# One instruction per pair of heads for the score maxima and the exponentials, on one PSUM tile; a third pair of W2 tiles split earlier

## The chip, the cores and the metric

The kernel runs on one core of a Trainium2 chip. The metric is device time in microseconds (us) of one execution; lower is better. Before the change it is 2239.94 us, the median of three runs between 2239.41 and 2240.25.

## What is computed

Two branches share one input and are mixed per token by a sigmoid gate: softmax attention with 32 heads of 18 channels, and an MLP with a hidden width of 4608.

```python
x = A_x                                            # (1, 2048, 576), float32
g = sigmoid((x * gate_w).sum(-1, keepdims=True))
q, k, v = heads(x @ wqkv)                          # 32 heads, Dh = 18
p = softmax(q @ k.T * 18 ** -0.5)
a = merge(p @ v) @ wo
b = gelu(layernorm(x) @ w1 + b1) @ w2 + b2         # 576 -> 4608 -> 576
out = g * a + (1 - g) * b
```

## The kernel before

**Three stages.** The entry stage (about 0 to 235 us) transposes x, forms the scores' operands q and k (`qk_group`) and v (`v_group`), stores them in DRAM scratch, and writes the normalised x for the MLP. It also runs the first rounds of score maxima and prepares the first MLP weights. The main loop (to about 2163 us) is attention, with the whole MLP cut into small pieces between its matmuls. A short end projects the attention output with `wo` and adds the gated MLP rows.

**The attention loop.** Heads are taken in 16 pairs and queries in halves, which makes 32 units of 16 steps, 512 steps in all. A matmul needs at most 64 of the array's 128 rows here, so the two heads of a pair lie in the upper and the lower rows, and their matmuls run side by side. Below, a *pair* is such a couple of score matmuls, head 0 then head 1, each writing 512 columns, one PSUM bank. A step issues four pairs in turn: `s2` (keys by queries, L271, whose scores ACT turns into exponentials, L275), `s1` (queries by keys for the unit after next, L226, whose row maxima DVE takes, L228), and the same again. Every two to four steps `pv` (L291) multiplies the stored exponentials by v in one burst. Between the pairs lie pieces of the MLP: `h_pair` (L539, hidden units) and `out_pair` (L627, output rows). Reading a bank out, by the maximum or the exponential, is called its *evacuation* below: only after it may the bank be written again.

**What sets the order.** The program's order on each engine is fixed when it is built. `half_round`, `fill` and `turn_ends` place pieces by nominal costs (231 and 131 ns a step), `run_due` releases work that `defer` has put off by so many slots, and the list `bg` holds weight splits, each of which starts once its load should have landed: `LOADED` is the slot of the load plus `LAND`. Each engine then runs its own list in order and waits on semaphores that the builder inserts wherever two accesses to the same memory must not be exchanged.

**PSUM.** There are eight banks. `score_bank` hands the score matmuls a ring of five in the loop (three of `ps_s1`, two of `ps_s2`) and of four in the entry stage (three of `ps_s1`, one of `ps_o`). `ps_w` has two for the MLP, `ps_o` one for the output of `pv`, `ps_a` four in the entry stage. Each bank is a tile of its own. With five banks and two for each pair, a matmul's bank was last used two or three pairs earlier: in the built program the nearest evacuation that a pair of score matmuls waits for is that of two pairs back for 2012 of the 2048 pairs.

**Weights.** `split` rounds a loaded W1 or W2 tile (ACT, L402, L403, L405) and subtracts the rounded part from it (POOL, called from `pool_op`, L179), so that two reduced-precision matmuls give a float32 product. The parts go to scratch, and later token blocks read them from there (`reload`, L421). W1 and W2 are split in the first token block; `prep` and `prep_w2` ask for it.

Of the kernel before, what the change touches and what calls it, by code (L numbers as in the profile page):

```python
# [8 lines left out]
F32 = mybir.dt.float32  # L9
F32R = mybir.dt.float32r  # L10
AF = mybir.ActivationFunctionType
ALU = mybir.AluOpType
# [20 lines left out]
GC0 = 1.0 / 0.044715  # L33
LN_EPS = 1e-5
HALF = S // 2
NS1 = 3
LEAD = 4
FILL = 1250.0
SLOT = 950.0
# [27 lines left out]
def gated_mix_kernel(ctx: ExitStack, tc: tile.TileContext, x, wqkv, wo, w1, b1, w2, b2, gate_w, out):  # L67
# [32 lines left out]
    pp = ctx.enter_context(tc.tile_pool(name="pp", bufs=2))  # L100
    hp = ctx.enter_context(tc.tile_pool(name="hp", bufs=6))
    asm = ctx.enter_context(tc.tile_pool(name="asm", bufs=2))
    ps_s1 = ctx.enter_context(tc.tile_pool(name="ps_s1", bufs=NS1, space=PSUM))
    ps_o = ctx.enter_context(tc.tile_pool(name="ps_o", bufs=1, space=PSUM))
    QA = [att.tile([P, HALF], F32R, name=f"qa{i}") for i in range(3)]
    KA = [att.tile([P, S], F32R, name=f"ka{i}") for i in range(2)]
    VT = [att.tile([P, NT, VW], F32, name=f"vt{i}") for i in range(2)]
# [1 line left out]
    V0 = att.tile([P, NT, VW], F32, name="v0")  # L109
    oe = att.tile([P, TB], F32, name="oe")  # L110

    def psum(pool):
        return pool.tile([P, TB], F32, name="ps")

    ring = [0]

    def score_bank():

        ring[0] += 1
        if not looped[0]:  # L120
            return psum(ps_s1 if ring[0] % (NS1 + 1) < NS1 else ps_o)
        return psum(ps_s1 if ring[0] % (NS1 + 2) < NS1 else ps_s2)

    def big_tile():
        return yp.tile([P, 9, TB], F32R, name="big")
# [62 lines left out]
    def unit(u):  # L188
        return UNITS[u]
# [26 lines left out]
    def s1_round(u, r):  # L216


        t, kb = (r % 8, r // 8) if u in (0, NU - 3) else divmod(r, 4)
        if r == 0:  # L220
            M4[u] = asm.tile([P, 2, 8, 4], F32, name="m4")
        qa, ka = QA[u % 3], KA[unit(u)[0] % 2]
        for h in range(2):
            r0 = 64 * h
            ps = score_bank()
            nc.tensor.matmul(ps, qa[r0:r0 + 54, t * P:(t + 1) * P], ka[r0:r0 + 54, kb * TB:(kb + 1) * TB],  # L226
                             start=True, stop=True)
            nc.vector.tensor_reduce(M4[u][:, h, t, kb:kb + 1], ps, axis=AX.X, op=ALU.max)  # L228

    def s1_finish(u):  # L230

# [31 lines left out]
    def s2(u, kc, qb):  # L263
        qa, ka = QA[u % 3], KA[unit(u)[0] % 2]
        n = u * NT + kc
        if n < 2 and qb == 0:
            RING.insert(n, pp.tile([P, 2, 2, TB], F32, name="p"))
        ps = [score_bank() for _ in range(2)]
        for h in range(2):
            r0 = 64 * h  # L270
            nc.tensor.matmul(ps[h], ka[r0:r0 + 56, kc * P:(kc + 1) * P], qa[r0:r0 + 56, qb * TB:(qb + 1) * TB],  # L271
                             start=True, stop=True)
        def exps():
            for h in range(2):
                nc.scalar.activation(p_of(n)[:, qb, h], ps[h], AF.Exp, scale=SCALE)  # L275
        return exps

    OB = {}
# [1 line left out]
    def pv(n, m):  # L280

        u, kc = divmod(n, NT)
        if kc == 0:
            OB[u] = psum(ps_o)
        v = v_of(unit(u)[0])
        for c in range(n, n + m):
            for qb in range(2):
                for h in range(2):
                    r = 32 * (2 * h + qb)
                    k = c % NT  # L290
                    nc.tensor.matmul(OB[u][r:r + 32, :], v[:, k, 19 * h:19 * h + 32], p_of(c)[:, qb, h, :],  # L291
                                     start=(k == 0), stop=(k == NT - 1))
        if kc + m == NT:
            o_store(u, OB.pop(u))
# [45 lines left out]
    def mlp():  # L340
# [26 lines left out]
        def load_w1(q):  # L367

            if (1, q) in LOADED or q >= NQ0:
                return  # L370
            LOADED[1, q] = slot[0] + LAND
            f0 = 2 * q * P
            raw = raw1(q)
            for h in range(2):
                src = w1[256 * h:256 * h + 256, f0:f0 + 2 * P].rearrange("(c p) n -> p c n", p=64)
                nc.sync.dma_start(raw[64 * h:64 * h + 64, 0:8].rearrange("p (c j) n -> p c (j n)", j=2), src)
            for h in range(2):
                for j in range(2):
                    f1 = f0 + (j ^ h) * P
                    nc.sync.dma_start(raw[64 * h:64 * h + 64, 8 + j], w1[512:576, f1:f1 + P])  # L380

        def load_w2(c):
            if (2, c) in LOADED or c >= NFC:
                return
            LOADED[2, c] = slot[0] + LAND
            nc.sync.dma_start(raw2(c), w2[c * P:(c + 1) * P, :])

        def rounded(dst, src):
# [58 lines left out]
        room = [6]  # L447
        w2_next = [0]

        def prep_w2(upto):  # L450

            late = 0
            while room[0] and w2_next[0] < 2 * min(upto, npair):
                q, j = divmod(w2_next[0], 2)
                w2_next[0] += 1
                if last_of(of[q][0]) and q >= npair - 3 and q < npair - 1:
                    continue
                room[0] -= 1
                c = 2 * (q % NQ0) + j
                if q >= NQ0:  # L460
                    defer(late, lambda q=q, j=j, c=c: reload(W2, (q, j), wp2, [P, 2, D], w2_scr[c]))
                    late += 2
                    continue
                split(W2, (q, j), wp2, [P, 2, D], (2, c), raw2(c), w2_scr[c],
                      lambda c: load_w2(c + 2))
# [48 lines left out]
        def h_pair(q, inner=False):  # L514
# [6 lines left out]
                yield 0  # L521
            wh, wl = ready(W1, q)
            del W1[q]
            ps = [psum(ps_w) for _ in range(2)]
# [79 lines left out]
        def out_pair(i, t, acc):  # L604
# [4 lines left out]
            ps = [psum(ps_w) for _ in range(2)]  # L609
            steps = 12 * size  # L610
            ends = turn_ends(steps, steps // 2, {4: 1.5})
            k = 0
# [97 lines left out]
        for i in range(n + 1):  # L710
            q = first_of[i] if i < n else 0
            if i < n:
                yield from pair(q)
            if i > 0:
                if i == n:
                    between = {}
                elif last_of(i) and seq[i][2] > 2:
                    between = {0: pair(q + 1), 1: pair(q + 2, inner=True)}
                else:
                    between = {0 if seq[i][2] == 2 else 1: pair(q + 1)}  # L720
                was = held[0]
# [48 lines left out]
    with ExitStack() as a:  # L770
        wpool = a.enter_context(tc.tile_pool(name="a_w", bufs=1, side="right"))
        sm = a.enter_context(tc.tile_pool(name="a_sm", bufs=2, side="right"))
        ps_a = a.enter_context(tc.tile_pool(name="ps_a", bufs=4, space=PSUM))

        qkstack = ExitStack()
        wqk = qkstack.enter_context(tc.tile_pool(name="a_wqk", bufs=1))
# [41 lines left out]
                eng.tensor_tensor(lo[:, cs], raw[:, cs], hi[:, cs].bitcast(F32), op=ALU.subtract)  # L818

        def transposed(tb, c):  # L820
            ps = psum(ps_a)
# [66 lines left out]

        def stat_rows(tb):

            ps = psum(ps_a)
# [47 lines left out]
        def qk_group(tb, mt):  # L939
            big = xT[tb]  # L940
            wh, wl = W_QK
            ms = slice(mt * P, (mt + 1) * P)
            ps = psum(ps_a)
            k = 0
            for c in range(4):
                for w_, s_ in ((wh, c), (wh, 4 + c), (wl, c)):
# [12 lines left out]
        def v_group(tb, t, n, between=None):  # L959
# [4 lines left out]
            ps = psum(ps_a)  # L964
            k = 0
            for c in range(4):
                for s_, w_ in ((c, wh), (c, wl), (4 + c, wh)):
# [36 lines left out]
        for tb in range(NB):  # L1004
            work = [(qk_group, (tb, mt)) for mt in (range(9) if tb < 2 else (4, 0, 1, 2, 3, 5, 6, 7, 8))] + [(v_group, (tb, t, n)) for t in range(4) for n in range(2)]
            for g, (fn, args) in enumerate(work):
# [35 lines left out]
                if tb == NB - 1:  # L1042
                    if g == 0:
                        next(stream[0])
                    if g == 1:
                        load_k(0, 3 * TB, S)
                    if g == 2:
                        load_q(1)
                        next(stream[0])
                    if g == 9:  # L1050
                        qkstack.close()
                        wp1 = mstack.enter_context(tc.tile_pool(name="m_w1", bufs=3))
                        wp2 = mstack.enter_context(tc.tile_pool(name="m_w2", bufs=6))
                        next(stream[0])
                    if g == 7:
                        ps = psum(ps_a)
                        nc.tensor.transpose(ps[:, :NFC], b1r, ident[:NFC, :NFC])
                        nc.vector.tensor_copy(b1t, ps[:, :NFC])
                if tb == 1 and g == 5:
# [30 lines left out]
    def out_proj():  # L1090
# [171 lines left out]
        for b in range(NB):  # L1262
# [6 lines left out]
            for t in range(4):  # L1269
# [5 lines left out]
                res = io.tile([P, D], F32, name="res", bufs=6)  # L1275
                for n in range(2):
                    cs = slice(n * ND, (n + 1) * ND)
                    ps = psum(ps_w)
                    k = 0
                    for c in range(5):  # L1280
                        while done[b] <= c:
# [125 lines left out]
```

## Time and profile before

| | |
|---|---|
| median of the runs | 2239.94 us |
| the profiled execution | 2238.79 us |
| its span, first to last instruction | 2237.0 us |
| PE (TensorE matmul) busy | 99% of the span |
| DVE (VectorE) busy | 72% |
| ACT (ScalarE) busy | 63% |
| POOL (GpSimd) busy | 45% |
| mean TensorE clock granted | 0.994 |

The span is 1.8 us shorter than the profiled execution's own time, and that time lies 1.15 us under the median. In the profile's rows PEld is TensorE's weight load, SP the engine that issues most DMAs, and L226 line 226 of the kernel above. A matmul's end is modelled, so a busy PE isn't PE at its peak; starts are recorded.

### The profile page before, as it was taken

What the parts mean: (1) busy time and instruction counts of PE and PEld (TensorE: products, weight loads), DVE (VectorE), ACT (ScalarE), POOL (GpSimd) and SP (SyncE); (2) the same over time, 40 slices, a digit from 0 to 9 for tenths busy, and PEclk for the clock granted to TensorE, in tenths of its full rate; (3) what the DMA queues carried; (4) which work ended last, traced back from release to release, by engine and by line L of the source; (5) the groups of instructions that cost most, each with busy time, mean ns of one, the idle gap of its engine ahead of it and who ended that gap; (6) DMA issues with size and microseconds to landing.
All of it is one profiled execution on the core that took longest, in us unless ns stands there. A gap on an engine that the chain in (4) does not pass through costs nothing.

```text
span 2237.0 us, 51358 instructions
## 1 busy us (share of the span) xinstructions
PE 2204.4 (99%) x20496; PEld 1620.0 (72%) x20496; DVE 1619.0 (72%) x2816; ACT 1418.5 (63%) x2636; POOL 1005.0 (45%) x1017
## 2 busy tenths in 40 slices
PE   8999999999999999999999999999999999999999
PEld 7877666767677777777767677777677777777768
DVE  6675766777777777777777777777777777777734
ACT  4323866767776666666765676666666666667672
POOL 4322765556554525434543452543535354254600
PEclk9999999999999999999999999999999999999999
DMA  8857646444453522342341533243344324323355
GB/s 265 273 205 240 216 149 191 148 152 157 145 166 120 181 101 97 125 138 94 125 138 58 171 142 111 91 141 125 107 131 156 118 85 150 110 91 124 124 171 167
DMA packets 162041, 324.36 MB, mean 145 GB/s; under 512 B 65830, under 2 KB 85218, under 8 KB 151074
## 3 DMA queue, kind: packets, MB, share of 16 engines
q1 hardware_dynamic: 159494, 317.61, 44.1%
q8 instruction: 161, 2.64, 0.5%
q10 hardware_dynamic: 2244, 3.45, 0.4%
q14 instruction: 78, 0.64, 0.1%
q0 software_dynamic: 64, 0.02, 0.0%
HBM read 228.62 MB, written 96.69 MB: 145 GB/s over the span
## 4 chain that ended last, share of the span: by engine, by line
PE 86%; DMA 4%; DVE 4%; POOL 2%; issue 2%; SPq 1%; ACT 1%; POOLq 0%; ACTq 0%; DVEq 0%
PE ps L291 19%; PE ps L627 19%; PE ps L539 18%; PE ps L271 12%; PE ps L226 10%; PE ps L947 3%; PE ps L1284 2%; DVE m L228 2%; DMA x<-in_B_w_dram 1%; PE ps L968 1%; POOL zz L179 1%; POOL w L179 1%; DMA bt<-b_scr 1%; SPq L380 1%; DMA x<-ot_scr 0%
## 5 line engine op out<-in xcount | busy, mean ns | idle before, releaser
L228 DVE TENSOR_REDUCE m<-ps 128x1 f32<-128x512 f32 x2048 | 1302.5, 684 | 450.7 <-PE ps L226 428.8
L275 ACT ACTIVATE p<-ps 128x512 f32<-128x512 f32 x1048 | 567.5, 597 | 305.8 <-PE ps L271 277.3
L275 ACT ACTIVATE ring<-ps 128x512 f32<-128x512 f32 x1000 | 542.4, 596 | 273.1 <-PE ps L271 263.7
L539 PE MATMUL ps<-big,w 64*128 64x512 f32 x3888 | 612.7, 393 | 0.2 <-issue 0.2
L179 POOL TENSOR_SCALAR zz<-zz 128x512 f32<-128x512 f32 x288 | 178.2, 619 | 726.3 <-ACT zz L599 670.9
L271 PE MATMUL ps<-qa,ka 56*128 56x512 f32 x2048 | 474.2, 421 | 6.7 <-ACT ring L275 3.0
L226 PE MATMUL ps<-ka,qa 54*128 54x512 f32 x2048 | 461.1, 403 | 7.4 <-DVE m L228 7.3
L539 PEld LDWEIGHTS ps<-big,w 64*128 64x128 f32 x3888 | 412.1, 187 | 51.4 <-DMA big<-y_scr 0.5
L179 POOL TENSOR_TENSOR zz<-zz,z 128x512 f32<-128x512 f32 x288 | 371.2, 1289 | 24.0
L271 PEld LDWEIGHTS ps<-qa,ka 56*128 56x128 f32 x2048 | 220.8, 185 | 198.2 <-DVE m L228 124.0
L627 PE MATMUL ps<-w,hh 64*128 64x288 f32 x2752 | 317.9, 296 | 1.2 <-DMA w<-w_scr 1.2
L627 PEld LDWEIGHTS ps<-w,hh 64*128 64x128 f32 x2752 | 277.8, 188 | 15.7 <-POOL zz L179 1.0
L226 PEld LDWEIGHTS ps<-ka,qa 54*128 54x128 f32 x2048 | 245.9, 185 | 39.0 <-DVE m L228 14.2
L291 PE MATMUL ps<-p,vt 128*32 128x512 f32 x1968 | 240.7, 597 | 0.0
L627 PE MATMUL ps<-w,big 64*128 64x288 f32 x2496 | 234.0, 294 | 3.4 <-ACT w L405 2.5
L627 PE MATMUL ps<-w,hl 64*128 64x288 f32 x1376 | 233.1, 294 | 0.0
L291 PE MATMUL ps<-ring,vt 128*32 128x512 f32 x1872 | 231.3, 596 | 0.0
L627 PEld LDWEIGHTS ps<-w,big 64*128 64x128 f32 x2496 | 218.7, 188 | 13.9 <-ACT w L405 2.8
L179 POOL TENSOR_TENSOR w<-x,w 128x1024 fp32r<-128x1024 f32 (+1 forms) x72 | 101.3, 1429 | 211.7 <-ACT w L402 120.2
L627 PEld LDWEIGHTS ps<-w,hl 64*128 64x128 f32 x1376 | 159.3, 187 | 0.2
L291 PEld LDWEIGHTS ps<-p,vt 128*32 128x32 f32 x1968 | 54.5, 109 | 116.3 <-issue 107.9
L291 PEld LDWEIGHTS ps<-ring,vt 128*32 128x32 f32 x1872 | 52.5, 109 | 115.1 <-issue 115.1
(126 smaller groups left out, 1715.8 us busy)
## 6 DMA issues: line engine op xcount, KB each, us to landing
w<-w_scr SPq DMA_DIRECT2D x54, 1152.0 KB
w<-w_scr SPq DMA_DIRECT2D x108, 576.0 KB
w_scr<-w SPq DMA_DIRECT2D x18, 1152.0 KB
w_scr<-w SPq DMA_DIRECT2D x36, 576.0 KB
qa<-qk_scr SPq DMA_DIRECT2D x192, 72.0 KB
ka<-qk_scr SPq DMA_DIRECT2D x84, 144.0 KB
x<-in_B_w_dram SPq DMA_DIRECT2D x36, 288.0 KB
qk_scr<-hh SPq DMA_DIRECT2D x36, 256.0 KB
```

The lines of the kernel that those rows point to most:

```text
L179: fn(*args, **kw)
L226: nc.tensor.matmul(ps, qa[r0:r0 + 54, t * P:(t + 1) * P], ka[r0:r0 + 54, kb * TB:(kb + 1) * TB], start=True, stop=True)
L228: nc.vector.tensor_reduce(M4[u][:, h, t, kb:kb + 1], ps, axis=AX.X, op=ALU.max)
L271: nc.tensor.matmul(ps[h], ka[r0:r0 + 56, kc * P:(kc + 1) * P], qa[r0:r0 + 56, qb * TB:(qb + 1) * TB], start=True, stop=True)
L275: nc.scalar.activation(p_of(n)[:, qb, h], ps[h], AF.Exp, scale=SCALE)
L291: nc.tensor.matmul(OB[u][r:r + 32, :], v[:, k, 19 * h:19 * h + 32], p_of(c)[:, qb, h, :], start=(k == 0), stop=(k == NT - 1))
L380: nc.sync.dma_start(raw[64 * h:64 * h + 64, 8 + j], w1[512:576, f1:f1 + P])
L539: mm = nc.tensor.matmul(ps[nn], w_[r, 2 * c + nn if c < 4 else 8], y, start=(k == 0), stop=(k == 26))
L627: mm = nc.tensor.matmul(ps[nn][:, :ND], h_[r, tok], w_[p_][r, cs[nn]], start=(k == 0), stop=(k == steps - 1))
L947: nc.tensor.matmul(ps, w_[:, c, ms], big[:, s_, :], start=(k == 0), stop=False)
L968: nc.tensor.matmul(ps[:, :ND], big[:, s_, tok], w_[:, c, cs], start=(k == 0), stop=False)
L1284: nc.tensor.matmul(ps[:, :ND], OT[b][2][:, s_, tok], w_part(w_, c)[:, cs], start=(k == 0), stop=(k == 13))
```

## The change

All of PSUM becomes one tile of eight banks, `PS`, and a table says which banks each use takes in turn. `score_banks` takes the next two banks of the ring and returns them as one strided slice, with the lower bank first. In the loop the ring is 0, 1, 2, 3, 4, so the slices are (0,1), (2,3), (0,4), (1,2), (3,4), and then (0,1) again; in the entry stage they are (0,1) and (2,5). `s1_round` takes both heads' maxima in one reduce of 2 x 512 elements, `s2` both heads' exponentials in one activation. The names of the pools and the rings change accordingly; the lines move down by one or two.

In the weights, `prep_w2(3)` adds the third pair of W2 tiles to those split in the entry stage, a load in the loop counts as landed four slots later, and in the last group of a token block the reloads of W2 are one slot apart, not two.

```diff
-    ps_s1 = ctx.enter_context(tc.tile_pool(name="ps_s1", bufs=NS1, space=PSUM))
-    ps_o = ctx.enter_context(tc.tile_pool(name="ps_o", bufs=1, space=PSUM))
+    PS = ctx.enter_context(tc.tile_pool(name="ps", bufs=1, space=PSUM)).tile([P, 8, TB], F32, name="ps")
...
-    def score_bank():
-
-        ring[0] += 1
-        if not looped[0]:
-            return psum(ps_s1 if ring[0] % (NS1 + 1) < NS1 else ps_o)
-        return psum(ps_s1 if ring[0] % (NS1 + 2) < NS1 else ps_s2)
+    BANKS = {"s": (0, 1, 2, 5), "a": (3, 4, 6, 7), "o": (5,), "w": (6, 7)}
+    given = {}
+
+    def bank(use):
+
+        given[use] = given.get(use, -1) + 1
+        return BANKS[use][given[use] % len(BANKS[use])]
+
+    def psum(use):
+        return PS[:, bank(use)]
+
+    def score_banks():
+
+        lo, hi = sorted((bank("s"), bank("s")))
+        return PS[:, lo:hi + 1:hi - lo]
...
+        ps = score_banks()
         for h in range(2):
             r0 = 64 * h
-            ps = score_bank()
-            nc.tensor.matmul(ps, qa[r0:r0 + 54, t * P:(t + 1) * P], ka[r0:r0 + 54, kb * TB:(kb + 1) * TB],
+            nc.tensor.matmul(ps[:, h], qa[r0:r0 + 54, t * P:(t + 1) * P], ka[r0:r0 + 54, kb * TB:(kb + 1) * TB],
                              start=True, stop=True)
-            nc.vector.tensor_reduce(M4[u][:, h, t, kb:kb + 1], ps, axis=AX.X, op=ALU.max)
+        nc.vector.tensor_reduce(M4[u][:, :, t, kb], ps, axis=AX.X, op=ALU.max)
...
-        ps = [score_bank() for _ in range(2)]
+        ps = score_banks()
...
-            for h in range(2):
-                nc.scalar.activation(p_of(n)[:, qb, h], ps[h], AF.Exp, scale=SCALE)
+            nc.scalar.activation(p_of(n)[:, qb], ps, AF.Exp, scale=SCALE)
...
-            LOADED[1, q] = slot[0] + LAND
+            LOADED[1, q] = slot[0] + LAND + 4 * looped[0]
...
-            LOADED[2, c] = slot[0] + LAND
+            LOADED[2, c] = slot[0] + LAND + 4 * looped[0]
...
-        def prep_w2(upto):
+        def prep_w2(upto, apart=2):
...
-                    late += 2
+                    late += apart
...
         prep_w2(2)
         prep(2)
+        prep_w2(3)
...
-                    prep_w2(first_of[i] + seq[i][2] + 2 * (seq[i][0] == 0 and not last_of(i)))
+                    prep_w2(first_of[i] + seq[i][2] + 2 * (seq[i][0] == 0 and not last_of(i)), 1 if last_of(i) else 2)
...
-    ps_s2 = ctx.enter_context(tc.tile_pool(name="ps_s2", bufs=2, space=PSUM))
-    ps_w = ctx.enter_context(tc.tile_pool(name="ps_w", bufs=2, space=PSUM))
+    BANKS["s"] = (0, 1, 2, 3, 4)
+    given["s"] = -1
```

The order of PE's matmuls is the same in both programs, instruction by instruction. What differs on PE is what they wait for. The first place is PE in the loop, at 743.4 to 745 us of the profile of before: a pair of `s1`, a pair of `s2` and a pair of `s1`, with pieces of `out_pair` between. `ps` is a score bank, `hh` and `hl` are the parts of a hidden tile, and `[waits ...]` names the engine whose count the instruction waits for. Before:

```order
L226 MATMUL ps<-ka_108,qa_105 128x512 [waits Activation_49]
L226 MATMUL ps<-ka_108,qa_105 128x512 [waits DVE_49]
L627 MATMUL ps<-w_9559,hh 128x288 x4
L627 MATMUL ps<-w_9559,hl 128x288 x2
L271 MATMUL ps<-qa_107,ka_108 128x512 [waits DVE_49]
L271 MATMUL ps<-qa_107,ka_108 128x512 [waits Activation_49]
```

And in the changed program:

```order
L228 MATMUL ps<-ka_106,qa_103 128x512 [waits DVE_49]
L228 MATMUL ps<-ka_106,qa_103 128x512
L628 MATMUL ps<-w_7780,hh 128x288 x4
L628 MATMUL ps<-w_7780,hl 128x288 x2
L273 MATMUL ps<-qa_105,ka_106 128x512 [waits DVE_49]
L273 MATMUL ps<-qa_105,ka_106 128x512 [waits Activation_49]
```

No matmul has moved. The first `s1` pair here has the banks (0,4), the `s2` pair after it the banks (1,2). Before, the count for which the first L271 waits was that of the reduce three pairs back; now the count for which the first L273 waits is reached only by the reduce of the `s1` pair just ahead of it, the one that reads the slice (0,4). Such a wait, for the evacuation of the pair immediately ahead, stands before 392 of the 2048 pairs of the changed program, each time where a pair in (1,2) follows one in (0,4); before it stood before 10.

The second place is DVE at the same part of the loop, its reduces (`m` is the tile of maxima) and the sums of `out_pair`. Before:

```order
L228 TENSOR_REDUCE m_9806<-ps 128x1 [waits PE_49] x8
L640 SCALAR_TENSOR_TENSOR x<-ps,x 128x288 [waits PE_49] x2
L228 TENSOR_REDUCE m_9806<-ps 128x1 [waits PE_49] x6
```

And now:

```order
L230 TENSOR_REDUCE m_7974<-ps 128x2 [waits PE_49]
L641 SCALAR_TENSOR_TENSOR x<-ps,x 128x288 [waits PE_49] x2
L230 TENSOR_REDUCE m_7974<-ps 128x2 [waits PE_49,Activation_49] x2
L230 TENSOR_REDUCE m_7974<-ps 128x2 [waits PE_49]
L230 TENSOR_REDUCE m_7974<-ps 128x2 [waits PE_49,Activation_49]
```

Two reduces have become one, and some of them now wait for ACT as well as for PE. In 378 reduces that count is reached only by the exponential of the pair immediately ahead, and 377 exponentials wait likewise for the reduce of the pair ahead; before, a score evacuation waited for no evacuation on the other engine. In the entry stage 17 groups (of `qk_group`, `v_group` and the transposes, in the banks 3 and 4) wait for the reduce of a pair in (2,5).

The third place is POOL at the end of the entry stage, its share of the weight splits (`x` the loaded tile, `w` the rounded one: 128x576 a W2 tile, 128x1024 and 128x128 a W1 tile). Before:

```order
L179 TENSOR_TENSOR w_2278<-x,w_2278 128x1024
L179 TENSOR_TENSOR w_2278<-x,w_2278 128x128
L179 TENSOR_TENSOR w_2453<-x,w_2453 128x1024
L179 TENSOR_TENSOR w_2453<-x,w_2453 128x128
L179 TENSOR_SCALAR zz<-zz 128x512
```

And now:

```order
L181 TENSOR_TENSOR w_2065<-x,w_2065 128x1024
L181 TENSOR_TENSOR w_2065<-x,w_2065 128x128
L181 TENSOR_TENSOR w_2133<-x,w_2133 128x576
L181 TENSOR_TENSOR w_2164<-x,w_2164 128x576
L181 TENSOR_TENSOR w_2213<-x,w_2213 128x1024
L181 TENSOR_TENSOR w_2213<-x,w_2213 128x128
```

Two W2 subtractions have come forward, ahead of the third W1 tile; their two ACT roundings, two loads and two stores have come with them. In the first token block most later W2 splits stand one GELU piece further back than before.

More of the change, by code (lines that the diff above doesn't have):

```diff
@@ L35 @@
 HALF = S // 2
-NS1 = 3
 LEAD = 4
@@ L110, in gated_mix_kernel @@
     oe = att.tile([P, TB], F32, name="oe")
-    def psum(pool):
-        return pool.tile([P, TB], F32, name="ps")
-    ring = [0]
-    def score_bank():
-        ring[0] += 1
-        if not looped[0]:
-            return psum(ps_s1 if ring[0] % (NS1 + 1) < NS1 else ps_o)
-        return psum(ps_s1 if ring[0] % (NS1 + 2) < NS1 else ps_s2)
+    BANKS = {"s": (0, 1, 2, 5), "a": (3, 4, 6, 7), "o": (5,), "w": (6, 7)}
[8 more added lines that the diff above has]
+        return PS[:, lo:hi + 1:hi - lo]
     def big_tile():
@@ L267, in s2 @@
             RING.insert(n, pp.tile([P, 2, 2, TB], F32, name="p"))
-        ps = [score_bank() for _ in range(2)]
+        ps = score_banks()
         for h in range(2):
             r0 = 64 * h
-            nc.tensor.matmul(ps[h], ka[r0:r0 + 56, kc * P:(kc + 1) * P], qa[r0:r0 + 56, qb * TB:(qb + 1) * TB],
+            nc.tensor.matmul(ps[:, h], ka[r0:r0 + 56, kc * P:(kc + 1) * P], qa[r0:r0 + 56, qb * TB:(qb + 1) * TB],
                              start=True, stop=True)
         def exps():
-            for h in range(2):
-                nc.scalar.activation(p_of(n)[:, qb, h], ps[h], AF.Exp, scale=SCALE)
+            nc.scalar.activation(p_of(n)[:, qb], ps, AF.Exp, scale=SCALE)
         return exps
@@ L283, in pv @@
         if kc == 0:
-            OB[u] = psum(ps_o)
+            OB[u] = psum("o")
         v = v_of(unit(u)[0])
@@ L523, in h_pair @@
             del W1[q]
-            ps = [psum(ps_w) for _ in range(2)]
+            ps = [psum("w") for _ in range(2)]
             change = tb + 1 < NB and (q + 1) % NQ0 == 0
@@ L608, in out_pair @@
             cs = [slice(nn * ND, (nn + 1) * ND) for nn in range(2)]
-            ps = [psum(ps_w) for _ in range(2)]
+            ps = [psum("w") for _ in range(2)]
             steps = 12 * size
@@ L772, in gated_mix_kernel @@
         sm = a.enter_context(tc.tile_pool(name="a_sm", bufs=2, side="right"))
-        ps_a = a.enter_context(tc.tile_pool(name="ps_a", bufs=4, space=PSUM))
         qkstack = ExitStack()
@@ L820, in transposed @@
         def transposed(tb, c):
-            ps = psum(ps_a)
+            ps = psum("a")
             for t in range(4):
@@ L889, in stat_rows @@
         def stat_rows(tb):
-            ps = psum(ps_a)
+            ps = psum("a")
             nc.tensor.transpose(ps[:, :P], stp, ident)
@@ L942, in qk_group @@
             ms = slice(mt * P, (mt + 1) * P)
-            ps = psum(ps_a)
+            ps = psum("a")
             k = 0
@@ L963, in v_group @@
             wh, wl = W_V
-            ps = psum(ps_a)
+            ps = psum("a")
             k = 0
@@ L1055, in gated_mix_kernel @@
                     if g == 7:
-                        ps = psum(ps_a)
+                        ps = psum("a")
                         nc.tensor.transpose(ps[:, :NFC], b1r, ident[:NFC, :NFC])
@@ L1277, in out_proj @@
                     cs = slice(n * ND, (n + 1) * ND)
-                    ps = psum(ps_w)
+                    ps = psum("w")
                     k = 0
```

## The prediction

> **What bounds the kernel now.** First the page's head, its busy slices and its chain.
>
> ```profile
> span 2237.0 us, 51358 instructions
> PE   8999999999999999999999999999999999999999
> PE 86%; DMA 4%; DVE 4%; POOL 2%; issue 2%; SPq 1%; ACT 1%; POOLq 0%; ACTq 0%; DVEq 0%
> ```
>
> PE is busy in every slice and makes up 86% of the chain that ended last. Whatever this change makes of DVE and ACT therefore counts only where PE waits for them. The waits, PE's alone, show how often it does now:
>
> ```profile
> PE ps L226 <- DVE m L228: 7.3, 9, 1.6
> PE ps L271 <- ACT ring L275: 3.0, 2, 2.4
> PE ps L627 <- ACT w L405: 2.5, 1, 2.5
> PE ps L271 <- ACT p L275: 2.0, 2, 1.4
> PE ps L271 <- DVE m L228: 0.8, 1, 0.8
> ```
>
> The columns are the total, the times and the longest. Score matmuls wait 13.1 us for evacuations in the whole kernel (7.3 + 3.0 + 2.0 + 0.8). That is all that a faster evacuation can return there. What a later one can cost depends on how closely pairs follow each other. The stretches below are 240 to 2160 us, three times, for the matmuls of `s1`, of `s2` and of `pv`:
>
> ```profile
> 240.00:2160.00 1920.00, 438.83 (x1942) 235.51 (x1942) 0.99 0.41 131
> 240.00:2160.00 1920.00, 460.90 (x1988) 215.03 (x1988) 0.99 0.41 131
> 240.00:2160.00 1920.00, 465.57 (x4000) 111.31 (x3992) 0.99 0.41 131
> ```
>
> Two matmuls make a pair, so (1942 + 1988) / 2 = 1965 pairs start in 1920 us, of which `pv` takes 465.6. Outside its bursts a pair follows the last one after (1920 − 465.6) / 1965 = **0.74 us**, and two pairs span 1.48 us.
>
> **The change part by part: what one evacuation costs.** The place of the first order rows:
>
> ```profile
> 742.15 0.41 PE L226 MATMUL ps<-ka,qa 54*128 54x512 f32 x2
> 742.39 0.42 PE L271 MATMUL ps<-qa,ka 56*128 56x512 f32 x2
> 742.59 2.58 DVE L228 TENSOR_REDUCE m<-ps 128x1 f32<-128x512 f32 x4 [0.37 <-PE ps L226]
> 742.85 1.09 ACT L275 ACTIVATE ring<-ps 128x512 f32<-128x512 f32 x2 [0.21 <-PE ps L271]
> 743.43 0.42 PE L226 MATMUL ps<-ka,qa 54*128 54x512 f32 x2
> 744.07 0.41 PE L271 MATMUL ps<-qa,ka 56*128 56x512 f32 x2
> ```
>
> The reduce starts 0.44 us after its matmuls start (742.59 − 742.15), the exponential 0.46 (742.85 − 742.39); I take 0.45 for both. Two reduces take 1.29 us (half of 2.58), two exponentials 1.09. A merged instruction isn't in this trace. Groups of one kind in two sizes give its price:
>
> ```profile
> L302 DVE COPY oe<-ps 128x512 f32<-128x512 f32 x32 | 22.1, 692 | 19.1 <-PE ps L291 18.0
> L979 DVE COPY vt<-ps 128x288 f32<-128x288 f32 x16 | 7.3, 454 | 5.9 <-PE ps L971 5.9
> L402 ACT ACTIVATE w<-x 128x1152 fp32r<-128x1152 f32 x18 | 21.0, 1167 | 0.3 <-DMA v_scr<-vt 0.3
> L405 ACT ACTIVATE w<-x 128x576 fp32r<-128x576 f32 x36 | 23.5, 685 | 13.0 <-DMA x<-in_B_w_dram 13.0
> L228 DVE TENSOR_REDUCE m<-ps 128x1 f32<-128x512 f32 x2048 | 1302.5, 684 | 450.7 <-PE ps L226 428.8
> L275 ACT ACTIVATE p<-ps 128x512 f32<-128x512 f32 x1048 | 567.5, 597 | 305.8 <-PE ps L271 277.3
> ```
>
> DVE: (692 − 454) / 224 = 1.06 ns an element, so the merged reduce is 684 + 512 × 1.06 = 1.23 us. ACT: (1167 − 685) / 576 = 0.84, so the merged exponential is 597 + 512 × 0.84 = 1.03 us. Rows bound them by two single ones (1.29 and 1.09) and by one (0.68 and 0.60); that floor would mean 512 elements for nothing, which both slopes exclude. At ACT's slope the reduce would be 1.11; for the exponential I allow 0.08 below, 0.95, an estimate. Both engines get some 0.06 us a pair back, but **the bank that used to come free after the first 0.68 or 0.60 us comes free only after 1.23 or 1.03**. How fast PE goes on once released:
>
> ```profile
> 315.92 0.68 ACT L405 ACTIVATE w<-x 128x576 fp32r<-128x576 f32 x1 [1.86 <-DMA x<-in_B_w_dram]
> 316.65 0.60 PE L627 MATMUL ps<-w,big 64*128 64x288 f32 x2 [2.54 <-ACT w L405]
> 316.68 1.40 POOL L179 TENSOR_TENSOR w<-x,w 128x576 fp32r<-128x576 f32 x1
> 318.13 1.57 PE L627 MATMUL ps<-w,big 64*128 64x288 f32 x10 [0.87 <-POOL w L179]
> ```
>
> ACT ends at 316.60 and PE starts at 316.65; POOL ends at 318.08, PE starts at 318.13: 0.05 us, twice. I use it between DVE and ACT too.
>
> **Term 1, the wait for the pair immediately ahead.** The slice (0,4) is strided from bank 0 to bank 4, and the built waits treat it as if it covered all five. So its evacuation waits for that of the pair in (2,3), and the pair in (1,2) waits for its evacuation, though it shares no bank with it. On PE, the pair in (2,3) starts at 0; its evacuation starts at 0.45 and ends at 1.68 (DVE) or 1.48 (ACT); 0.05 later the other engine begins and ends at 0.45 + 1.23 + 0.05 + 1.03 = 2.76 either way; the pair in (1,2) can start at 2.81. In today's order it starts at 1.48: **1.33 us lost**. Behind the waiting matmul stand all MLP pieces and `pv`, PE being in order, so nothing hides it but a `pv` burst that lies between the three pairs. The weight load after a burst counts these:
>
> ```profile
> PEld ps L271 <- DVE m L228: 124.0, 180, 1.1
> ```
>
> 180 bursts on 1965 gaps: 9.2% a gap, 18.3% for two. Of 392 such waits 392 × 0.817 = 320 cost 1.33 us: **+426 us**. With the low durations (1.11 and 0.95) the loss is 1.13 and the term 362; with the high ones 1.45 and 464.
>
> **Term 2, the honest waits.** In a cycle of five pairs, three more wait for the evacuation two pairs back (the fourth, in (3,4), waits for the (0,4) that is already done). It needs 0.45 + 1.23 + 0.05 = 1.73 us for a reduce, 1.53 for an exponential, against 1.48: 0.25 and 0.05, in the mean 0.15. 3 × 320 × 0.15 = **+144 us**. In today's form the first half is free at 0.45 + 0.68 + 0.05 = 1.18, and no pair needs to wait. Low durations give 0.13 and nothing, 62 us; pairs 0.64 apart, as at 743.43 and 744.07, give 0.45 and 0.25, 336 us.
>
> **Term 3, the entry stage.** One of the 17 groups that wait for a reduce in (2,5):
>
> ```profile
> 181.52 0.74 PE L226 MATMUL ps<-ka,qa 54*128 54x512 f32 x4
> 182.19 3.06 PE L947 MATMUL ps<-big,wqk 128*128 128x512 f32 x12
> 182.91 2.47 DVE L228 TENSOR_REDUCE m<-ps 128x1 f32<-128x512 f32 x4
> ```
>
> Two merged reduces from 182.91 end at 185.37, so L947 starts at 185.42, not 182.19: 3.2 us. Where the (2,5) pair isn't the last thing ahead it is less, down to nothing; I take 2.0 in the mean: **+34 us** (20 to 50).
>
> **Term 4, the clock.** Three stretches around a long stall, and one shortly stalled:
>
> ```profile
> core 0: us, PE busy (x) PEld busy (x) DVE busy (x) ACT busy (x) POOL busy (x), PEclk, DMA share, GB/s
> 589.45:592.87 3.42, 1.87 (x14) 0.99 (x12) 3.39 (x6) 0.80 (x3) 1.03 (x1) 1.00 0.52 154
> 592.87:596.28 3.41, 3.41 (x20) 2.66 (x18) 1.55 (x3) 1.07 (x3) 0.00 (x0) 0.50 0.94 316
> 1572.40:1575.80 3.40, 2.72 (x35) 2.30 (x31) 3.26 (x7) 2.97 (x6) 2.60 (x3) 1.00 0.06 21
> 1575.80:1579.20 3.40, 3.02 (x33) 2.58 (x35) 2.97 (x6) 1.93 (x4) 3.13 (x4) 1.00 0.07 13
> ```
>
> Busy for 1.87 of 3.42 us, PE ran the next 3.41 us at half clock, which loses 1.7 us; busy for 2.72 of 3.40 it didn't. A stretch with one stall of 1.33 us is busy for about 2.1 of 3.4, between the two. I take half clock after ten of the entry's stalls and five in the loop, 15 × 1.7 = **+25 us** (0 to 60). The Trainium skill, "TensorE: Matmul & The Clock Gate", Part 1, lets the clock fall after an idle window of about 3.4 us; by that no stall of 1.33 us would ever do it, and the term would be nearly 0. The row at 589.45 speaks against it: its window was more than half busy.
>
> **Returned.** The 13 us of evacuation waits are contained in the terms: −13. The third W2 pair's earlier split takes away the wait at 316.65 (2.54, then 0.87 us) and the half clock after it; the later-counted loads may spare ACT some of the 13.0 us that L405 waits for DMA. The two further POOL subtractions and ACT roundings in the entry lie beside other work there. I take **−15 us** (0 to −25). The single reload slot stands where no PE wait is seen: 0. Merging saves ACT and DVE about 60 us each, off the path: 0.
>
> **The sum**, on the profiled execution's 2238.8 us (its span and 1.8 around it): 2238.8 + 426 + 144 + 34 + 25 − 13 − 15 = **2840 us**, 27% above the median of 2239.94. All low ends: 2238.8 + 362 + 62 + 20 − 13 − 25 = 2645. All high ends: 2238.8 + 464 + 336 + 50 + 60 − 13 = 3136.
>
> **Rivals.** *Only real bank sharing counts.* Were the pair in (1,2) released without the evacuation of (0,4), each pair would have only term 2, five in a cycle: 5 × 320 × 0.15 = 240, and 2238.8 + 240 − 28 = about 2450. For it: those slices share no bank. The Trainium skill, "PSUM — Partial Sum Buffer", section on bank collisions, asks for semaphores by bank and quadrant, by which (0,4) and (1,2) need none. Against it: the wait stands in the built program, and hardware obeys it. *The clock gives way.* If most stalled stretches fall to half clock, each of 320 cycles loses up to 1.7 us and gets about half back because its waits then fit: about +270, 3100 us. For it: 1.87 of 3.42 was enough. Against it: 2.72 wasn't. *Not slower.* One mechanism: evacuations end before they are wanted, because PE, not the bank, sets the pace. It decides from pairs 1.4 us apart, half of 2.81; then only the returned 28 us are left, 2212 us. For it: PE waits 13.1 us today. Against it: pairs are 0.74 apart, and that 13.1 holds only because half a pair's banks come free early. That the merge isn't done at all is excluded by the order rows.
>
> **How the numbers follow.** The forecast, both kinds of wait, 0.83; the clock 0.08; only real sharing 0.05; not slower 0.04, of which 0.03 is faster and 0.01 the same. A difference of 0.2%, some 4.5 us, is about what a measurement of this kernel can tell from none. Slower is 0.96 less 0.01 for some overlap that I don't see, which goes to the same: 0.95 slower, 0.02 same, 0.03 faster. The range is 2640 to 3050: the low end of the sum, and two thirds of the way to its high end, which needs every price at its worst.
>
> **What would show it.** Right: one reduce of about 1.23 us and one exponential of about 1.03; PE waits for DVE and ACT at L228 and L273 of some 500 us in place of 13, some 300 of them over 1 us; PE busy near 80%. Reduces that start right at the end of an exponential show the first link of term 1. Wrong: the same count of long waits at a smaller size (the merged instructions are shorter), a PEclk row with many dips (the clock), or waits of 0.1 to 0.3 us alone (only real sharing).

## The result and the profile after

The changed kernel takes 2969.26 us, the median of four runs (2965.01 to 2976.31), against 2239.68 before: 1.326 times as long, with a 95% interval of 1.3235 to 1.3288. The forecast was 2840, in a range of 2640 to 3050. The head of the page of the changed kernel, its busy slices, the clock granted and the chain:

```profile
span 2967.2 us, 50030 instructions
PE   9887888888888888888888888888888887888899
PEclk9899999999999999999999999999999999999999
DVE m L230 20%; PE ps L292 16%; PE ps L228 13%; PE ps L273 10%; PE ps L540 9%; PE ps L628 9%; ACT p L276 5%; ACT ring L276 4%; PE ps L948 2%; PE ps L1285 1%; PE ps L969 1%; DMA x<-ot_scr 0%; DMA qa<-qk_scr 0%; DMA bt<-b_scr 0%; DMA ka<-qk_scr 0%
```

PE was busy in every slice; now a tenth or two is missing throughout the loop, and the maxima (L230, 20%) and exponentials (L276, 9%) stand in the chain that PE had almost to itself. The same as waits, PE's own rows:

```profile
PE ps L273 <- DVE m L230: 178.9, 162, 1.7
PE ps L228 <- ACT ring L276: 97.3, 94, 1.7
PE ps L228 <- ACT p L276: 90.0, 92, 1.8
PE ps L228 <- DVE m L230: 35.5, 137, 1.0
PE ps L948 <- DVE m L230: 15.3, 5, 3.3
PE ps L969 <- DVE m L230: 12.2, 6, 3.1
```

The 13 us that score matmuls waited have become 402 in the first four rows. (The prediction looked for some 500, with some 300 of the waits over 1 us; 188 are. PE is busy for 84% of the span, where it said near 80%.) The first three are the pattern of the strided slice: `s2` waits for the maximum, `s1` for the exponential, each the engine of the *other* kind, hence of the pair just ahead, by about 1 us a time. The fourth is `s1` waiting for its own kind, two pairs back, by 0.26 us a time. The last two are groups of the entry stage. A stall's first part still counts as busy here, since ends are modelled, so these rows are less than what was lost.

The merged instructions, in the groups:

```profile
L230 DVE TENSOR_REDUCE m<-ps 128x2 f32<-128x1024 f32 x1024 | 1251.7, 1224 | 1123.7 <-PE ps L228 1000.4
L276 ACT ACTIVATE p<-ps 128x1024 f32<-128x1024 f32 x524 | 536.7, 1025 | 661.8 <-PE ps L273 520.0
```

1.22 and 1.03 us, as the two slopes gave (1.23 and 1.03). DVE and ACT are indeed relieved, by 51 and 61 us (from 1302.5 and 1109.9). They spend it waiting.

The place at 743 us of before lies at 954 us now (timeline, same instructions):

```profile
954.01 0.65 PE L228 MATMUL ps<-ka,qa 54*128 54x512 f32 x2
954.25 0.74 PE L273 MATMUL ps<-qa,ka 56*128 56x512 f32 x2
954.69 1.23 DVE L230 TENSOR_REDUCE m<-ps 128x2 f32<-128x1024 f32 x1 [0.59 <-PE ps L273]
955.03 1.02 ACT L276 ACTIVATE ring<-ps 128x1024 f32<-128x1024 f32 x1 [0.58 <-PE ps L628]
955.97 0.19 PEld L228 LDWEIGHTS ps<-ka,qa 54*128 54x128 f32 x2 [0.42 <-DVE m L230]
955.97 0.50 PE L228 MATMUL ps<-ka,qa 54*128 54x512 f32 x2 [0.19 <-DVE m L230]
956.58 1.23 DVE L230 TENSOR_REDUCE m<-ps 128x2 f32<-128x1024 f32 x1 [0.67 <-PE ps L228]
957.86 0.51 PE L273 MATMUL ps<-qa,ka 56*128 56x512 f32 x2 [0.99 <-DVE m L230]
958.61 0.40 PE L228 MATMUL ps<-ka,qa 54*128 54x512 f32 x2
```

Both kinds of wait are here. The L228 at 955.97 waits two pairs back: the reduce ends at 955.92. It is the pair in (0,4). The L273 at 957.86 is the pair in (1,2) and starts 0.05 us after the reduce of that (0,4) slice, at 957.81. Before, these two pairs were 0.64 us apart (743.43 and 744.07); now it is 1.89. The reduce at 956.58 starts 0.61 us after its stalled matmuls, not 0.44. Their weight load (PEld) starts only with them, at 955.97; before, the load for the pair at 743.43 had started 0.11 us ahead of it:

```profile
743.32 0.20 PEld L226 LDWEIGHTS ps<-ka,qa 54*128 54x128 f32 x2
```

That the late load is what delays the reduce is read from these rows; no run tried it alone.

PE's matmuls stand in the same order in both programs, so the distance of each pair from the one ahead can be compared one by one. Summed over the traces: 391 of the loop's 401 pairs in (1,2), all but one of those with a wait for the pair immediately ahead, come 452 us later in all, by 1.25 us in the median; the pair after each, 36 us (0.1 us each); the other three of the cycle, 183 us (188 in two of them, a little under nothing in the third); the entry stage, 49 us. That is 720 of the 730 us between the spans; the rest lies at the few loop pairs left out.

### The profile page after: what moved, and what is told of

It reads as the page before. It is cut to its first block, busy times and chain, and to the rows that moved or that the text cites. A ratio compares the mean times of both kernels' runs of the same rounds, so it can differ in the third digit from the quotient of the medians.

```text
span 2967.2 us, 50030 instructions
## 1 busy us (share of the span) xinstructions
PE 2506.6 (84%) x20496; PEld 1631.1 (55%) x20496; DVE 1575.4 (53%) x1792; ACT 1365.8 (46%) x1612; POOL 1002.4 (34%) x1017
## 4 chain that ended last, share of the span: by engine, by line
PE 60%; DVE 21%; ACT 10%; issue 3%; DMA 1%; SPq 0%; DVEq 0%; ACTq 0%; POOL 0%; POOLq 0%
DVE m L230 20%; PE ps L292 16%; PE ps L228 13%; PE ps L273 10%; PE ps L540 9%; PE ps L628 9%; ACT p L276 5%; ACT ring L276 4%; PE ps L948 2%; PE ps L1285 1%; PE ps L969 1%; DMA x<-ot_scr 0%; DMA qa<-qk_scr 0%; DMA bt<-b_scr 0%; DMA ka<-qk_scr 0%
## 5 line engine op out<-in xcount | busy, mean ns | idle before, releaser
L230 DVE TENSOR_REDUCE m<-ps 128x2 f32<-128x1024 f32 x1024 | 1251.7, 1224 | 1123.7 <-PE ps L228 1000.4
L276 ACT ACTIVATE p<-ps 128x1024 f32<-128x1024 f32 x524 | 536.7, 1025 | 661.8 <-PE ps L273 520.0
L276 ACT ACTIVATE ring<-ps 128x1024 f32<-128x1024 f32 x500 | 512.3, 1025 | 657.7 <-PE ps L273 536.3
L228 PE MATMUL ps<-ka,qa 54*128 54x512 f32 x2048 | 569.7, 447 | 229.6 <-ACT ring L276 97.3
L273 PE MATMUL ps<-qa,ka 56*128 56x512 f32 x2048 | 541.6, 450 | 187.4 <-DVE m L230 178.9
L540 PE MATMUL ps<-big,w 64*128 64x512 f32 x3888 | 645.7, 400 | 0.0
L273 PEld LDWEIGHTS ps<-qa,ka 56*128 56x128 f32 x2048 | 250.3, 186 | 473.2 <-DVE m L230 249.9
L228 PEld LDWEIGHTS ps<-ka,qa 54*128 54x128 f32 x2048 | 252.9, 187 | 426.7 <-DVE m L230 152.2
L628 PE MATMUL ps<-w,hh 64*128 64x288 f32 x2752 | 332.7, 296 | 0.0
L292 PE MATMUL ps<-p,vt 128*32 128x512 f32 x1968 | 254.5, 627 | 0.0
L948 PE MATMUL ps<-big,wqk 128*128 128x512 f32 x432 | 116.9, 422 | 16.3 <-DVE m L230 15.3
```

The source lines that it names most:

```text
L228: nc.tensor.matmul(ps[:, h], qa[r0:r0 + 54, t * P:(t + 1) * P], ka[r0:r0 + 54, kb * TB:(kb + 1) * TB], start=True, stop=True)
L230: nc.vector.tensor_reduce(M4[u][:, :, t, kb], ps, axis=AX.X, op=ALU.max)
L273: nc.tensor.matmul(ps[:, h], ka[r0:r0 + 56, kc * P:(kc + 1) * P], qa[r0:r0 + 56, qb * TB:(qb + 1) * TB], start=True, stop=True)
L276: nc.scalar.activation(p_of(n)[:, qb], ps, AF.Exp, scale=SCALE)
L540: mm = nc.tensor.matmul(ps[nn], w_[r, 2 * c + nn if c < 4 else 8], y, start=(k == 0), stop=(k == 26))
L628: mm = nc.tensor.matmul(ps[nn][:, :ND], h_[r, tok], w_[p_][r, cs[nn]], start=(k == 0), stop=(k == steps - 1))
```

## The experiments

**All of the merge undone, and three halfway houses.** `adj` reads a pair by one instruction only where its banks adjoin, `two` never does, `ring4` changes the ring so that they always adjoin, `boxes` so that they never do. The edits are in `score_banks`, the two reading places, and the ring. For `adj` and `two` (`two` has `if False` in both places):

```diff
-        return PS[:, lo:hi + 1:hi - lo]
+        return PS[:, lo:hi + 1:hi - lo], hi - lo == 1
...
-        nc.vector.tensor_reduce(M4[u][:, :, t, kb], ps, axis=AX.X, op=ALU.max)
+        if adjoin:
+            nc.vector.tensor_reduce(M4[u][:, :, t, kb], ps, axis=AX.X, op=ALU.max)
+        else:
+            for h in range(2):
+                nc.vector.tensor_reduce(M4[u][:, h, t, kb:kb + 1], ps[:, h], axis=AX.X, op=ALU.max)
```

and likewise for the exponentials. For `ring4` (the first new ring) and `boxes` (the second), from the changed kernel, with the entry stage's (2,5) read by two instructions:

```diff
-    BANKS["s"] = (0, 1, 2, 3, 4)
+    BANKS["s"] = (0, 1, 2, 3)
...
+    BANKS["s"] = (0, 2, 4, 1, 3)
```

> Maxima and exponentials are merged only where the two banks adjoin; a pair in the banks 0 and 4 (and 2 and 5 in the entry stage) is read by two instructions, so no strided slice is read at all and no pair waits for the pair immediately ahead. Theory (the wait through the slice (0,4) is the largest part, the later release of merged banks the second): the 452 us before pairs with such a wait and the 49 us of the entry stage go, term 2 stays at all five pairs of a cycle: 2460 to 2560 us, best guess 2500. Rival 1 (the length of the merged evacuation does nearly all of it, whatever the slice): above 2800. Rival 2 (waits two pairs back cost nothing by themselves): below 2300.

> One PSUM tile, the bank tables and the edits of the weights as in the changed kernel, but every bank is read by an instruction of its own, 2048 reduces and 2048 exponentials. Theory: all of the loss is in the merged reads, so the time is that of before or a little under it, 2205 to 2245 us (the weights' edits may return up to 25). Rival (the single PSUM tile by itself brings waits, or the edits of the weights cost): above 2300.

> All pairs merged in the loop, but on a ring of four banks, (0,1) and (2,3) in turn, so that merged slices always adjoin; bank 4 stays unused; the slice (2,5) of the entry stage is read by two instructions. Theory: no wait for the pair immediately ahead although every evacuation is merged; each pair waits two pairs back, 1.73 us for a maximum and 1.53 for an exponential against 1.48: 2470 to 2620 us, although there is one bank less than in the changed kernel. Rival (the merged reads cost by their length or the number of banks, not by the slice): as slow as the changed kernel or slower, 2950 and up.

> As the changed kernel, but the loop's ring is 0, 2, 4, 1, 3, so that the slices are (0,2), (1,4), (0,3), (2,4), (1,3): each one's stretch from its lower to its upper bank overlaps the one before, though no two neighbours share a bank. Theory: nearly every pair (1954 of 2048) now waits for the evacuation immediately ahead, so that pairs follow each other by 0.45 + 1.13 + 0.05 = 1.63 us in place of 0.74 wherever no burst lies between: about 0.89 us on some 1750 pairs, 3650 to 3950 us. Rival (the wait through the stretch between the banks is not what costs): within 5% of the changed kernel, 2820 to 3120.

Measured, the kernel before at 2237.58 us: `adj` 2549.49 (ratio 1.139, 1.137 to 1.142), `ring4` 2517.94 (1.125, 1.123 to 1.127), `two` 2298.02 (1.027, 1.025 to 1.029), `boxes` 4495.91 (2.008, 2.003 to 2.014; two executions). `adj` and `ring4` lie in their ranges.

`ring4` decides the main point: with every evacuation merged and a bank *less*, it is 451 us faster than the changed kernel, of which 46 belong to the entry stage (`entry_two`, below). Neither the length of the merged read nor the number of banks is what costs most, but the slice that reaches from bank 0 to bank 4. `boxes` is the counter-test: in the loop the same instructions on the same five banks, in another order, cost 1527 us more than the changed kernel. It overshot the upper end of its forecast by some 550 us, and its page shows a loss that the forecast lacked:

```profile
span 4490.5 us, 49547 instructions
PEclk9967777777777776676676666677667676777779
```

The granted clock is 0.734 in the mean, 187 half-clock stretches of 2394 us in all. Set against the same pairs of the kernel before, those that follow the pair ahead wholly at full clock come 0.68 us later in the mean, those wholly at half clock 1.27; the forecast, 0.89 us on 1750 pairs, is 0.78 for each of the loop's 2008. This is what the rival "the clock gives way" of the prediction describes: it happens in `boxes`, and hardly in the changed kernel (a mean clock of 0.976).

`two` missed both sides of its expectation: 60 us slower than before although no merged read was left. Pair by pair, 56 us of it stood at one pair in five, the one behind the pair in (3,4). `score_banks` sorts the banks, so the pair that the ring gives (4,0) has head 0 in bank 0 and head 1 in bank 4. Bank 4 is wanted again two pairs later, bank 0 three; before, the earlier reading freed bank 4, now the later one does. It is the second matmul of the pair in (3,4) that waits for it, so the loss shows at the next pair: that matmul starts 0.24 us after the first in the mean, against 0.05 before.

**The order of the heads, and the weights.** `two_ring` is `two` with the ring's order kept; `weights` is the kernel before with the edits of the weights alone.

```diff
-        lo, hi = sorted((bank("s"), bank("s")))
-        return PS[:, lo:hi + 1:hi - lo], hi - lo == 1
+        b0, b1 = bank("s"), bank("s")
+        return [PS[:, b0], PS[:, b1]], PS[:, b0:b0 + 2] if b1 == b0 + 1 else None
```

> As 'two', but a pair that gets the banks 4 and 0 keeps the ring's order, head 0 in bank 4 and head 1 in bank 0, as before the change; 'two' sorted them, so that head 1 of the pair two further on waited for the second reading of the two. Theory: that order is all of the 60 us by which 'two' was slower than before, since its loss stands at one pair in five; the time falls to 2210 to 2245 us. Rival (the single PSUM tile or the weights' edits cost): it stays near 2298.

> The kernel before with the edits of the weights alone: the third W2 pair split in the entry stage, loads counted as landed four slots later, reloads one slot apart in the last groups. Theory: they return 0 to 25 us by removing the wait at 316 us and its half clock: 2210 to 2240. Rival (they cost, and explain part of 'two'): 2250 to 2300.

Measured, before at 2238.79: `two_ring` 2222.81 (0.9932, 0.9918 to 0.9945), `weights` 2218.37 (0.9907, 0.9895 to 0.9920). The order of two heads was worth 75 us. One PSUM tile instead of pools costs at most the 4 us between these two, little more than the executions of one kernel differ by. The weight loads of `s1` in `two` and in `two_ring`, first `two`:

```profile
PEld ps L228 <- DVE m L234: 65.8, 147, 2.0
```

and `two_ring`:

```profile
PEld ps L228 <- DVE m L234: 12.6, 20, 2.0
```

147 waits became 20. `weights` beats both kernels of the case by taking away stalls of the first token block, and with them four of the five stretches of half clock of before. One is that at 316 us; the timeline of `weights` there:

```profile
314.93 0.69 ACT L405 ACTIVATE w<-x 128x576 fp32r<-128x576 f32 x1
315.55 0.57 PE L627 MATMUL ps<-w,big 64*128 64x288 f32 x6
316.17 0.74 PE L627 MATMUL ps<-w,big 64*128 64x288 f32 x5
```

The W2 tile whose rounding PE awaited is ready from the entry stage, and L627 runs on beside the splits of later tiles. But by 355 us, past this place, only 6.6 of the 21 us between the two traces are returned. The rest comes at about 377, 436, 490 and 593 us of before. At 377 and 490 us ACT had waited 4.0 and 3.6 us for the load of a W2 tile, and PE then for the exponentials that stood behind its rounding. These waits of ACT for loads, first before, then in `weights`:

```profile
ACT w L405 <- DMA x<-in_B_w_dram: 13.0, 8, 4.0
ACT w L405 <- DMA x<-in_B_w_dram: 1.1, 2, 0.7
```

What the earlier split and the later-counted loads each did was not tried apart.

**One engine at a time.** `exp_ring` is `two_ring` with the exponentials merged where banks adjoin, `red_ring` with the maxima, `adj_ring` with both:

```diff
-            for h in range(2):
-                nc.scalar.activation(p_of(n)[:, qb, h], ps[h], AF.Exp, scale=SCALE)
+            if both is not None:
+                nc.scalar.activation(p_of(n)[:, qb], both, AF.Exp, scale=SCALE)
+            else:
+                for h in range(2):
+                    nc.scalar.activation(p_of(n)[:, qb, h], ps[h], AF.Exp, scale=SCALE)
```

> As 'two_ring', but the exponentials are merged where their two banks adjoin (four pairs in five); the maxima stay two instructions. Theory: an s2 pair now comes free after 0.45 + 1.03 + 0.05 = 1.53 us, against 1.48 between pairs two apart, so only closer pairs wait: 20 to 90 us over 'two_ring'. Rival (the merge gains, since ACT is relieved): at or below 'two_ring'.

> As 'two_ring', but the maxima are merged where their two banks adjoin; the exponentials stay two instructions. Theory: 0.45 + 1.23 + 0.05 = 1.73 us against 1.48, so most waiting pairs lose a quarter of a us: 100 to 220 us over 'two_ring', two to four times what the exponentials cost. Rival (both cost alike, because the later release matters and not its length): equal to 'exp_ring' within 20 us.

> As 'adj', maxima and exponentials merged where the banks adjoin, but the pair in the banks 4 and 0 keeps the ring's order. It holds every merged read of the changed kernel but the strided ones. 'exp_ring' lies 110 us over 'two_ring' (2222.8) and 'red_ring' 223. Theory: a wait for one engine also spreads the pairs for the other, so the two losses add to less than their sum: 2440 to 2545 us; what the changed kernel has above this is the price of its strided slices, some 420 to 530 us. Rival (the losses add): 2556 or more.

Measured: `exp_ring` 2332.72 (ratio 1.042, 1.041 to 1.044), `red_ring` 2446.30 (1.093, 1.091 to 1.094), `adj_ring` 2490.98 (1.1125, 1.110 to 1.115). Over `two_ring` the exponentials cost 110 us, the maxima 223, both together 268, less than the sum of 333. The order of sizes and the overlap were as expected. Both single ones were larger than their expectation (20 to 90, and 100 to 220). In `exp_ring`, the weight load of `s2`, which waits for the exponentials, shows how many pairs are caught:

```profile
PEld ps L277 <- ACT p L281: 66.1, 204, 0.6
PEld ps L277 <- ACT ring L281: 60.6, 179, 0.7
```

383 waits of a third of a us where a mean distance of 1.48 against 1.53 would have given 0.05 each. The clock plays no part: `adj_ring` ran at a granted 1.0.

**The entry stage alone.** `entry_two` is the changed kernel, with (2,5) read by two instructions (`if adjoin or looped[0]`).

> The changed kernel with one edit: in the entry stage the maxima of a pair in the banks 2 and 5 are taken by two instructions, so that no group in the banks 3 and 4 waits for them; the loop is as in the changed kernel. Theory: the entry stage's 49 us go, 2905 to 2935 us. Rival (they come back in the loop, where the loads are then late): above 2950.

Measured 2922.89 us (1.305, 1.302 to 1.308), 46 us under the changed kernel. The waits of the loop are as they were there, so nothing came back:

```profile
PE ps L277 <- DVE m L231: 179.0, 162, 1.9
PE ps L228 <- ACT ring L281: 96.6, 94, 1.6
PE ps L228 <- ACT p L281: 91.8, 92, 2.1
PE ps L228 <- DVE m L231: 33.5, 126, 1.0
```

Put in a row, the runs give the whole: before 2239; the weights' edits and the single tile, 2223 (−16); both readings merged where banks adjoin, 2491 (+268); the strided slices of the loop, 2923 (+432); those of the entry stage, 2969 (+46). The step of +432 changes the order of the heads of the pair in (0,4) too; against `adj`, which has the changed kernel's order and takes 2549, the strided slices of the loop cost 373.

## Why the prediction came out right

**What bounds it.** Right. PE waited for 13 us before, so faster evacuations had nothing to return there, and later ones cost time wherever a pair follows closely. The path was right; the forecast lies 129 us under the measured time because most terms were too small.

**The prices of the merged instructions.** Right to 0.01 us. **The release**: 0.05 us again, at 955.97 and 957.86.

**Term 1**, +426 forecast. The runs give 432 between `adj_ring` and `entry_two`, though that difference also holds (0,4)'s share of the other terms, and 373 between `adj` and `entry_two`; the trace gives 452 at the waiting pairs, 1.25 us in the median against 1.33 worked out. That the term came so close is in part luck: it counted 320 stalls, since bursts were to hide the others, and in the trace 355 of the 392 pairs start right at the release (about 0.05 us after the evacuation of (0,4)). More stalls, each a little cheaper, made nearly the same sum. That the wait comes from the stretch between the banks, not from a bank that is shared, is shown by `ring4`, `adj_ring` and, from the other side, `boxes`; *only real bank sharing counts* has fallen. That the builder takes a strided slice for its whole stretch was read from the waits of the built program, and no run contradicts it. The first link, one evacuation waiting for the other engine's, shows in the waits of the changed kernel:

```profile
ACT ring L276 <- DVE m L230: 87.8, 66, 2.3
ACT p L276 <- DVE m L230: 85.7, 61, 3.4
```

It often doesn't bind. Of the 355 stalls, 201 have an evacuation of (0,4) that starts within 0.1 us of the end of that of (2,3), as the working had it. In the other 154 it starts later, often because the pair in (0,4) had itself waited: at 956.58 the end of the exponential (956.05) was past, and the reduce had only its own stalled matmuls to wait for. There term 2's wait sets the start of term 1's.

**Term 2** was mis-sized: +144 forecast, 183 in the trace for the three pairs of the cycle, and 268 in `adj_ring`, where four of five readings are merged and none stalls for a strided slice (the rival's sum said 240 for five). The step that failed is the mean: 0.25 and 0.05 us were worked out for pairs 1.48 us apart. But in the trace of before a quarter of the pairs start no more than about 1.27 us after the one two ahead, and nearly half (47%) less than 1.48. A wait is lost at each close pair and never earned back at a far one, so the mean distance understates it; pairs 0.64 apart stood in the text, but as an upper bound only. Summed over the starts in the trace of before, pair by pair, what is missing to 1.53 us comes to 100 us for the exponentials and what is missing to 1.73 to 233 for the maxima; four fifths of these, as four pairs in five are merged there, are 80 and 187. `exp_ring` and `red_ring` measured 110 and 223, the start after a stall (next paragraph) included; what else makes the difference stays open.

**What the sum lacked** is the start after a stall: 36 us in the trace, 0.1 us at the pair behind each stalled one.

**Term 3**, +34: 46 by `entry_two`, 49 in the trace. The place shown then was priced at 3.2 us; one such wait in the trace of the changed kernel is

```profile
232.88 3.52 PE L948 MATMUL ps<-big,wqk 128*128 128x512 f32 x8 [3.10 <-DVE m L230]
```

The mean of 2.0 was a little low, and the clock, priced in term 4, is in the 46.

**Term 4**, +25. A mean clock of 0.976 is 142 us at half clock in the trace (37 stretches), against 28 before, so some 57 us more of PE time lost by it. Forecast were 15 falls more; there were 31, so this term was less than half of what came. This loss isn't added to the terms as measured above: it is in them.

**Returned**: −28 forecast, of which −13 were the waits of before and −15 the weights' edits; these gave −16 in `two_ring` and −20 in `weights` alone. Right for the weights, though the 316 us stall that the prediction put first gave the smaller part. *Not slower* had nothing more to give than this, as the prediction said.

## What to carry to other kernels

Merging two short reads of PSUM into one long read saved the readers 51 and 61 us here, which shortened nothing, and held the first bank for the whole length; where the matmuls come back for that bank soon after it is free, the writer pays, and it pays at the closest returns, not at the mean. Read the waits of the built program before timing a new access pattern: a strided slice over banks can make neighbours wait that share nothing with it, and a ring whose length isn't a multiple of the slice's makes such slices. Price a wait against the distribution of distances in the trace, and look at which of two buffers comes free first: swapping two heads cost 75 us here.

## What was not expected of the hardware

The clock fell after stretches that were far from idle. In `boxes` (the columns are the busy time of PE, PEld, DVE, ACT and POOL, then the granted clock):

```profile
992.68:996.09 3.41, 2.15 (x14) 1.34 (x15) 3.17 (x6) 1.32 (x2) 2.58 (x2) 1.00 0.80 183
996.09:999.50 3.41, 3.05 (x15) 1.95 (x12) 0.99 (x1) 1.02 (x1) 0.00 (x0) 0.50 0.89 306
1000.00:1003.41 3.41, 2.22 (x12) 1.59 (x12) 1.23 (x1) 1.02 (x1) 0.00 (x0) 0.50 0.98 370
1003.41:1006.82 3.41, 2.88 (x16) 1.79 (x14) 1.23 (x1) 0.00 (x0) 0.00 (x0) 0.50 0.49 193
1006.82:1010.24 3.42, 2.70 (x13) 1.17 (x9) 1.23 (x1) 1.02 (x1) 0.00 (x0) 0.50 0.00 0
```

PE was busy for 63% of the stretch before the fall (2.15 of 3.41 us). Ahead of most of the 187 falls of this trace it was busy for 53 to 64% of the last 3.41 us (leaving out the lowest and the highest tenth). From 1000 us on PE is busy for 65 to 84% of each stretch (2.22 of 3.41, 2.88 of 3.41), and half clock lasts over all three. These three shares overstate the work done, since a matmul takes longer at half clock: a score matmul took 0.40 us in the median of before (L271), and the one at 1005.03 here 0.62:

```profile
1005.03 0.62 PE L277 MATMUL ps<-qa,ka 56*128 56x512 f32 x1
```

The Trainium skill, "TensorE: Matmul & The Clock Gate", Part 1, names an idle window of some 3.4 us as what closes the gate; the row at 992.68 doesn't agree with it. What share of work it takes was not tried.
